# A routed mixture of experts: when rows are gathered, on GpSimd's queue, and four weight pieces in flight

## The chip, the cores and the metric

The kernel runs on one core of one Trainium2 chip. The metric is the device time of one execution in microseconds (us), lower is better. A core has five engines that matter here, each with its own instruction stream: TensorE (PE in the profile; PEld is its weight load), VectorE (DVE), ScalarE (ACT), GpSimd (POOL) and SyncE (SP). They meet at semaphores. Data move by DMA; SyncE issues those with fixed addresses, GpSimd those whose rows are picked by an index (gathers and scatters).

## The reference

Attention, then a mixture of experts on its result, then a feed-forward layer with a cosine:

```python
x = attention(q, k, v)                      # 2 x 768 tokens of 8 heads x 64 = 1536 x 512, a window of 16 and block sums
do_compute = x @ w_skip > 0                 # a token below is passed on as it is
logits = x[do_compute] @ w_gate             # 8 experts
e_idx, gate_w = argmax(logits), max(softmax(logits))
for e in range(8):                          # each token to one expert
    mask = e_idx == e
    y[mask] = gate_w[mask] * (relu(xc[mask] @ w1[e]) @ w2[e])    # 512 -> 1024 -> 512
x[do_compute] += y
h = x @ w_in                                # 512 -> 2048
out = (h * cos(h)) @ w_out                  # 2048 -> 512
```

All is float32. Which expert has how many tokens is known only on the chip. An expert's weights are two tiles of 2 MB.

## The kernel before

Attention goes first; beside it each tile of 128 tokens is routed, and its result rows are written to `xb`, an array in device memory. Then 36 small matmuls (`slots`, L575) sum, over the twelve tiles, which token stands in which slot of which expert; `slot_ids` makes the row indices of it. A slot that no token fills gets index 0.

An expert's tokens come in up to three gathers from `xb`. `xg` (`ex_gather`, with index `GIA`) is the first 32 rows, as 64 half rows of 256, 64 KB. `xo` (`ov_gather`, `GIS`) is 64 further rows of 512, 128 KB. `xm` (`many_gather`, `GIB`) is 128 further rows, 256 KB, gathered only inside a branch on the count, above 96. GpSimd issues all of them in program order through the helper `gather` (L623), and the scatters that write an expert's rows back through `scatter` (L627). The gathers of `xg0` and `xg1` go out ahead of the others. After the slots the program gathers `xg2`, `xo0`, `xm0`, `xg3`, `xo1`, `xm1`, and so on to `xo7`.

TensorE's order is fixed by the program. After the index work come the transposes of `xg0` (`turn_x`, L601), expert 0's first layer (`ex_w1`, L639), the remaining sums of `slots` (L575 again, 36 matmuls of three columns per expert), and the transposes of `xg1`. Small matmuls on a zero tile (`warm`, L169) stand at the program's start and ahead of the transposes of `xg0`. Then the loop over the experts: `ex_t` (transposes, and a copy on ScalarE), `ex_w1` of the next expert, `ex_x` (the transposes of `xg` of the one after that), `ex_w2` (L998), and `overflow`. `overflow` is a branch: above 32 tokens it transposes `xo` (L1014), above 96 it runs `full_tile` (L1058) on `xm`, and where a part is left `part_tile` (L1025) on `xo`. Between the experts gathers by `PERME` (`yload`) fetch finished rows for the last layer; the scatters of later experts into `xb` wait for these.

The weights come in pieces of 0.5 MB that SyncE issues (`load_piece`, L196), into a ring of eight 2 MB tiles. A piece waits until the piece three ahead of it (`AHEAD`, from the loop on five) has landed, or for a gather where one is given as `after`:

```python
        if after is None and len(pieces) >= ahead_of[-1]:
            after = pieces[-ahead_of[-1]]
        if after is not None:
            tc.add_manual_dep(d.ins, after.ins.name, SYNC, reason="pace")
```

After the experts comes the last layer (L1219 and on), TensorE work throughout.

Of the kernel before, what the change touches and what calls it, by code (L numbers as in the profile page):

```python
# [32 lines left out]
CAP = 32  # L33
XT = 128
YT = 64
# [84 lines left out]
def tile_kernel(ctx: ExitStack, tc: tile.TileContext, consts, qh, kh, vh, vw, w9, w1, w2, w_in, w_out, out):  # L120
# [44 lines left out]
    def warm(pool, tag, n, w=512):  # L165

        t = pool.tile([P, w], F32, tag=tag, name="warm")
        for _ in range(n):
            nc.tensor.matmul(t, wz[:, 0:P], wz[:, 0:w], start=True, stop=True)  # L169
# [506 lines left out]
    for u in range(4):  # L676
        load_w(u)
    warm(ps_t, "t", 27)
    warm(ps_t, "t", 12, 64)
    for i in range(NI - 1):  # L680
        fill, hot = (), None
        if i >= 8 and i % 2 == 0:
# [167 lines left out]
    slots(pib, lb, tail)  # L850
    slots(pic, lc, tail)
    warm(ps_s, "s", WN)
    warm(ps_s, "s", 56, 64)
    slot_ids(pib, idb)
    load_piece(slot_gi(idb, False, GIB), 1)
    slot_ids(pic, idc)
# [82 lines left out]

    xo = {}  # L940

    def ex_gather(e):
        xg.append(m1.tile([QA, 256], F32, name=f"xg{e}"))
        return gather(xg[e], GIA[:, e:e + 1], xb2)
# [11 lines left out]
    def many_gather(e):  # L956
        if e > 1:
            how_many(e)
        xm[e] = m2.tile([P, DM], F32, tag="xm", name="xm")
        with tc.If(cnts[e][0] > CAP + YT):  # L960
            apart(gather(xm[e], GIB[:, e:e + 1], xb), None, ("m", e % 2))

    def ex_x(e):
        xe[e] = m2.tile([P, P], F32, tag="xe", name="xe")
# [5 lines left out]
    def apart(d, to=None, key=None):  # L970

        for p, k in outs + inner:
            if key is None or k != key:
                tc.declare_no_dep(d.ins, p.ins, reason="every token has one slot of one expert")
        if to is not None:
            to.append((d, key))
        return d

# [3 lines left out]
    def ex_t(e):  # L982
        h = hs[e]
        pt = ps_l.tile([P, 2, P], F32, tag="p", name="pth")
        for s in range(2):
            nc.tensor.transpose(pt[:, s, :], h[:, s * P:(s + 1) * P], ident)
        hT = m2.tile([P, 2, P], F32, tag="hT", name="hT")
        nc.scalar.copy(out=hT, in_=pt)
        hs[e] = hT

    def ex_w2(e, hT, po, ns=range(8)):
# [306 lines left out]
    cv_load(0, 0, first_in)  # L1298
    load_piece(first_in)
    load_piece(ex_gather(2))  # L1300
    for e in range(2):
        load_piece(ov_gather(e))
        many_gather(e)
        load_piece(ex_gather(e + 3))
    for e in range(2, NE):
        if e + 3 < NE:
            load_piece(ex_gather(e + 3))
        load_piece(ov_gather(e))
        if e in (3, 5):
            cv_load(0, (e - 1) // 2)  # L1310
    while wq:
# [3 lines left out]
    for e in range(NE):  # L1315
# [4 lines left out]
        if e + 2 < NE:  # L1320
            ex_x(e + 2)
        do("B", e)
        if 0 < e < NE - 1:
            many_gather(e + 1)
        po = ps_g.tile([P, 256], F32, tag="g", name="po") if e == NE - 1 else ps_o.tile([P, 256], F32, tag="o", name="po")
# [205 lines left out]
```

## Time and profile before

| | us |
|---|---|
| median of 3 runs | 479.93 (478.94 to 479.98) |
| the profiled execution's own time | 479.16 |
| its span, first to last instruction | 477.2 |
| TensorE busy | 437.9 |
| VectorE, ScalarE, GpSimd busy | 301.2, 214.2, 142.5 |
| mean granted clock of TensorE | 0.977 |

The profile is of one execution, and times in it count from the first instruction. The time of a run is that of the whole execution, some 2 us more than the span. A row's idle time is that of its engine just ahead of the instruction, and the arrow names what ended it: an instruction of another engine, a DMA, an engine's own sequencer (PEq), or "issue", where nothing that is recorded ended it. "remote" is a signal whose sender the records don't give.

### The profile page before, as it was taken

To read this page: it belongs to the slowest core of one execution; us is meant where nothing else is said; L and a number is where in the kernel's file an instruction comes from. 1 tells how busy PE (TensorE), PEld (TensorE's weight loads), DVE (VectorE), ACT (ScalarE), POOL (GpSimd) and SP (SyncE) were. 2 spreads that over 40 slices of the span, in tenths; PEclk is the share of its full clock that TensorE was granted. 3 is DMA by queue.
4 is the path that set the end of the run, shared out by engine and by line. 5 is a ranking of instruction groups with operands and counts; after the bars stand their busy time and mean duration, and the time that the engine had idled before them with its cause. 6 is when DMAs were issued, how large, how long until landed. Compare 5 with 4: busy or idle time off the path is not lost.

```text
span 477.2 us, 9227 instructions
## 1 busy us (share of the span) xinstructions
PE 437.9 (92%) x3273; PEld 319.6 (67%) x3276; DVE 301.2 (63%) x842; ACT 214.2 (45%) x523; POOL 142.5 (30%) x170
## 2 busy tenths in 40 slices
PE   8899999509989897999999999999999999999994
PEld 4667676304444343567888888888888888888883
DVE  5697897106040051567679797998989956472831
ACT  2988993001332123346567566473646415051600
POOL 0755762650120024454053222231222100003043
PEclk9999999857999999999999999999999999999999
DMA  8999998799958389324312232321322000002021
GB/s 265 322 310 330 346 302 277 233 279 365 384 178 337 131 311 396 90 73 128 117 40 93 89 102 80 129 88 46 100 78 88 0 1 0 1 1 88 2 110 66
DMA packets 35180, 76.05 MB, mean 159 GB/s; under 512 B 4185, under 2 KB 10843, under 8 KB 35124
## 3 DMA queue, kind: packets, MB, share of 16 engines
q1 hardware_dynamic: 31876, 66.07, 42.2%
q0 software_dynamic: 3248, 9.27, 6.1%
q8 instruction: 31, 0.51, 0.5%
q14 instruction: 25, 0.20, 0.1%
HBM read 68.15 MB, written 7.60 MB: 159 GB/s over the span
## 4 chain that ended last, share of the span: by engine, by line
PE 29%; issue 18%; DVE 3%; POOL 3%; POOLq 0%; ACT 0%; DVEq 0%; ACTq 0%
PE pf L1219 14%; PE py L1398 11%; PE py L1464 2%; POOL out L627 2%; DVE g L1235 1%; PE pt L1144 1%; POOL wx L938 1%; DVE cvu L929 0%; DVE cvc L930 0%; DVE u L1225 0%; DVE c L1229 0%; POOLq L1527 0%; DVE nn L1224 0%; DVE cvu L927 0%; ACT u L1223 0%
## 5 line engine op out<-in xcount | busy, mean ns | idle before, releaser
L1219 PE MATMUL pf<-yb,wx 128*128 128x512 f32 x576 | 133.9, 390 | 1.3 <-DVE xg L1006 0.8
L1219 PEld LDWEIGHTS pf<-yb,wx 128*128 128x128 f32 x576 | 107.7, 188 | 24.2 <-PEq L1199 1.3
L1398 PE MATMUL py<-wx,g 128*128 128x512 f32 (+1 forms) x540 | 121.6, 384 | 0.0
L1398 PEld LDWEIGHTS py<-wx,g 128*128 128x128 f32 x540 | 99.9, 188 | 20.2
L1223 ACT ACTIVATE u<-pf,qbias 128x512 f32<-128x512 f32 x44 | 30.1, 685 | 78.2 <-PE pf L1219 78.0
L938 POOL TENSOR_TENSOR wx<-cvc,wx 128x512 fp32r<-128x512 f32 x24 | 34.7, 1446 | 94.7 <-ACT wx L937 91.5
L1404 DVE TENSOR_TENSOR ya<-py,ya 128x512 f32<-128x512 f32 (+1 forms) x37 | 23.8, 672 | 28.2 <-PE py L1398 26.2
L1235 DVE TENSOR_TENSOR g<-c,g 128x512 fp32r<-128x512 f32 x40 | 41.3, 1032 | 0.1
L336 ACT ACTIVATE sm<-sm,nm 128x128 f32<-128x128 f32 x96 | 37.4, 393 | 2.1 <-DVE nm L324 2.0
L1228 ACT ACTIVATE c<-u 128x512 f32<-128x512 f32 x44 | 27.6, 627 | 16.0 <-DVE g L1235 16.0
L627 POOL DMA_INDIRECT out<-ya,PERM x11 | 10.9, 992 | 79.9 <-DVE ya L1404 79.2
L1224 DVE TENSOR_SCALAR nn<-u 128x512 f32<-128x512 f32 x44 | 18.6, 424 | 23.1 <-ACT u L1223 23.0
L1225 DVE TENSOR_TENSOR u<-u,nn 128x512 f32<-128x512 f32 x44 | 30.5, 693 | 1.5
L1229 DVE TENSOR_TENSOR c<-pf,c 128x512 f32<-128x512 f32 x44 | 30.1, 684 | 0.7 <-ACT c L1228 0.7
L346 POOL TENSOR_TENSOR sm<-sm,su 128x512 f32<-128x512 f32 x23 | 24.2, 1050 | 21.3 <-DVE su L345 10.8
L324 DVE CUSTOM_DVE_ANT_0 sm<-sc,cst 128x128 f32<-128x128 f32 x96 | 23.6, 284 | 7.0 <-PE sc L317 6.0
L1234 ACT CAST g<-c 128x512 fp32r<-128x512 f32 x44 | 26.7, 607 | 0.2 <-DVE c L1229 0.2
L937 ACT CAST wx<-cvc 128x512 fp32r<-128x512 f32 x24 | 14.9, 622 | 16.1 <-DVE cvc L930 16.1
L1083 DVE SCALAR_TENSOR_TENSOR xm<-pox,GTB,xm 128x512 f32<-128x512 f32 x2 | 1.5, 750 | 30.4 <-PE pox L1073 30.4
L627 POOL DMA_INDIRECT xb<-xg,SIA x8 | 7.8, 978 | 41.9 <-DVEq L1199 15.5
L317 PE MATMUL sc<-kT,q 64*64 64x128 f32 x384 | 17.5, 282 | 2.3 <-DVE nm L324 1.4
L929 DVE SCALAR_TENSOR_TENSOR cvu<-cvc,cvu 128x512 int32<-128x512 int32 x24 | 17.5, 731 | 3.0 <-DVE cvu L927 0.5
(256 smaller groups left out, 631.5 us busy)
## 6 DMA issues: line engine op xcount, KB each, us to landing
w<-w SPq DMA_DIRECT2D x62, 512.0 KB
raw<-w_in SPq DMA_DIRECT2D x16, 512.0 KB
raw<-w_out SPq DMA_DIRECT2D x16, 512.0 KB
kT<-kh SPq DMA_DIRECT2D x8, 384.0 KB
vn<-vh SPq DMA_DIRECT2D x12, 256.0 KB
xb<-xtok SPq DMA_DIRECT2D x12, 256.0 KB
q<-qh SPq DMA_DIRECT2D x4, 512.0 KB
vt<-vw SPq DMA_DIRECT2D x12, 128.0 KB
```

The source lines that it names most:

```text
L336: nc.scalar.activation(out=sm[:, p, :], in_=sm[:, p, :], func=AF.Exp, scale=-1.0, bias=nm[:, p:p + 1], accum_out=su[:, p:p + 1])
L346: nc.gpsimd.tensor_tensor(out=sm, in0=sm, in1=su.unsqueeze(2).to_broadcast([P, NP, P]), op=ALU.mult)
L627: return nc.gpsimd.indirect_dma_start(out=dst, out_offset=bass.IndirectOffsetOnAxis(ap=idx, axis=0), in_=src, in_offset=None, bounds_check ...
L938: eng.tensor_tensor(out=lo, in0=c, in1=hi.bitcast(F32), op=ALU.subtract)
L1219: nc.tensor.matmul(p, w[:, k, fs], y[:, k, :], start=(n == 0), stop=(n == 11))
L1223: nc.scalar.activation(out=u, in_=p, func=AF.Identity, scale=1.0 / (2.0 * math.pi), bias=qbias)
L1225: nc.vector.tensor_tensor(out=u, in0=u, in1=nn, op=ALU.subtract)
L1228: nc.scalar.activation(out=c, in_=u, func=AF.Sin, scale=TWO_PI)
L1229: nc.vector.tensor_tensor(out=c, in0=p, in1=c, op=ALU.mult)
L1234: nc.scalar.copy(out=gh, in_=g)
L1235: (nc.gpsimd if i in POOL_G else nc.vector).tensor_tensor(out=gl, in0=g, in1=gh.bitcast(F32), op=ALU.subtract)
L1398: nc.tensor.matmul(p, a[:, ws], b[:, f, cs], start=(n == 0), stop=(n == 11))
```

## The change

Four things change. Twelve small warm-up matmuls move from ahead of the slots to the program's start. Among the gathers after the slots, `xg2`, `xg3` and `xg4` stay in a row with `xo1` and `xm1`, while `xg5`, `xg6` and `xg7` go out among the experts 1 and 2, behind the copy in `ex_t` (`begun`). `ov_gather` moves into `many_gather`, inside a branch on more than 32 tokens, an expert ahead of its use. The weight pieces after `xg3` wait only for other pieces, three back and then four back. Scatters no longer wait for gathers that are listed in `reads`, since no token has two slots.

```diff
-    warm(ps_t, "t", 12, 64)
+    warm(ps_t, "t", 24, 64)
...
-    warm(ps_s, "s", 56, 64)
+    warm(ps_s, "s", 44, 64)
...
+    begun = {}
+    reads = []
+
+    def behind(e, d):
+
+        if e > 0:
+            tc.add_manual_dep(d.ins, begun[e].ins.name, SYNC, reason="one expert after the other")
+        for p, _ in outs + inner:
+            tc.declare_no_dep(d.ins, p.ins, reason="every token has one slot of one expert")
+        reads.append(d)
+
...
         xm[e] = m2.tile([P, DM], F32, tag="xm", name="xm")
-        with tc.If(cnts[e][0] > CAP + YT):
-            apart(gather(xm[e], GIB[:, e:e + 1], xb), None, ("m", e % 2))
+        with tc.If(cnts[e][0] > CAP):
+            behind(e - 1, ov_gather(e))
+            with tc.If(cnts[e][0] > CAP + YT):
+                behind(e - 1, gather(xm[e], GIB[:, e:e + 1], xb))
...
         if to is not None:
+            for p in reads:
+                tc.declare_no_dep(d.ins, p.ins, reason="every token has one slot of one expert")
             to.append((d, key))
...
-        nc.scalar.copy(out=hT, in_=pt)
+        begun[e] = nc.scalar.copy(out=hT, in_=pt)
...
     load_piece(ex_gather(2))
-    for e in range(2):
-        load_piece(ov_gather(e))
-        many_gather(e)
-        load_piece(ex_gather(e + 3))
+    load_piece(ex_gather(3))
+    many_gather(0)
+    many_gather(1)
+    load_piece()
+    load_piece()
+    load_piece()
+    ahead_of.append(4)
     for e in range(2, NE):
         if e + 3 < NE:
-            load_piece(ex_gather(e + 3))
-        load_piece(ov_gather(e))
+            load_piece()
+        load_piece()
...
         do("B", e)
+        for g in {0: (4,), 1: (5,), 2: (6, 7)}.get(e, ()):
+            behind(e, ex_gather(g))
         if 0 < e < NE - 1:
             many_gather(e + 1)
```

The first place is on GpSimd, behind the slots. In the kernel before, from xg4 on (`xg_2092` is xg4, `xg_2095` xg5, `xo_2070` xo2, `xg_2100` xg6, `xo_2103` xo3, `xg_2108` xg7, `xo_2111` xo4, `xo_2114` xo5; the last row is xo6 and xo7, the scatter is that of expert 0):

```order
L623 DMA xg_2092<-xb,GIA 64x256
L623 DMA xg_2095<-xb,GIA 64x256
L623 DMA xo_2070<-xb,GIS 64x512
L623 DMA xg_2100<-xb,GIA 64x256
L623 DMA xo_2103<-xb,GIS 64x512
L623 DMA xg_2108<-xb,GIA 64x256
L623 DMA xo_2111<-xb,GIS 64x512
L623 DMA xo_2114<-xb,GIS 64x512
L623 DMA xo_2118<-xb,GIS 64x512 x2
L627 DMA xb<-xg_1774,SIA 3072x256
```

In the changed kernel, at the same place, from expert 1's branch on (L971 is the branch on 32 tokens, L973 that on 96; `xo_2069` is xo1, `xg_2157` xg4):

```order
L971 COMPARE_AND_BRANCH
L623 DMA xo_2069<-xb,GIS 64x512
L973 COMPARE_AND_BRANCH
L623 DMA xm<-xb,GIB 128x512
L973 UNCONDITIONAL_BRANCH
L973 ISA
L973 UNCONDITIONAL_BRANCH
L971 ISA
L971 UNCONDITIONAL_BRANCH
L623 DMA xg_2157<-xb,GIA 64x256
L627 DMA xb<-xg_1786,SIA 3072x256
```

After xg4 GpSimd goes on to the scatter of expert 0; nothing of the experts 5 to 7, and no `xo` of an expert beyond 1, stands ahead of it.

The second place is on GpSimd too, ahead of expert 5. In the kernel before, the last instruction of the scatters' branch of expert 3, the counts of expert 5 and the branch for its xm stand ahead of the scatter of xg4 (`xg_2092`):

```order
L1199 UNCONDITIONAL_BRANCH
L837 TENSOR_LOAD CNT x2
L960 COMPARE_AND_BRANCH
L623 DMA xm<-xb,GIB 128x512
L960 UNCONDITIONAL_BRANCH
L960 ISA
```

In the changed kernel (`xo_2912` is xo5), the same:

```order
L1214 UNCONDITIONAL_BRANCH
L837 TENSOR_LOAD CNT x2
L971 COMPARE_AND_BRANCH
L623 DMA xo_2912<-xb,GIS 64x512
L973 COMPARE_AND_BRANCH
L623 DMA xm<-xb,GIB 128x512
L973 UNCONDITIONAL_BRANCH
L973 ISA
```

The gather of xo5 has come from behind the slots to this place, behind the scatters of expert 3.

## Rows read from the trace of the kernel before

**Rows 1.** The page, part 1, first row: busy time, share of the span, instructions.

```profile
PE 437.9 (92%) x3273; PEld 319.6 (67%) x3276; DVE 301.2 (63%) x842; ACT 214.2 (45%) x523; POOL 142.5 (30%) x170
```

**Rows 2.** The page, part 4, first row: the chain that ended last, by engine.

```profile
PE 29%; issue 18%; DVE 3%; POOL 3%; POOLq 0%; ACT 0%; DVEq 0%; ACTq 0%
```

**Rows 3.** Stretch, length, busy PE, PEld, DVE, ACT, POOL; clock, DMA share, GB/s.

```profile
88.60:93.00 4.40, 1.40 (x26) 1.16 (x27) 0.00 (x0) 0.00 (x0) 3.18 (x5) 0.99 0.89 256
93.00:108.00 15.00, 1.76 (x12) 1.36 (x11) 0.10 (x1) 0.38 (x1) 8.74 (x10) 0.50 1.04 279
108.00:113.40 5.40, 5.40 (x48) 2.41 (x50) 3.45 (x26) 1.18 (x4) 0.00 (x0) 0.50 1.03 342
113.40:128.00 14.60, 14.26 (x127) 7.03 (x120) 5.63 (x25) 3.21 (x8) 1.95 (x2) 1.00 1.04 398
```

**Rows 4.** Timeline of TensorE (PE): start and length in us; idle before in brackets.

```profile
84.81 1.13 PE L169 MATMUL warm<-wz 128*128 128x64 bf16 x33
85.98 0.30 PE L601 MATMUL ptx<-ident,xg 64*128 64x64 f32 x2
86.64 1.93 PE L639 MATMUL ph<-w,cst 128*32 128x256 f32 x32 [0.35 <-ACT cst L602]
88.86 0.55 PE L575 MATMUL pia<-R,OR 128*64 128x24 bf16 x12 [0.29 <-issue]
...
99.34 0.18 PE L575 MATMUL pic<-R,OR 128*64 128x24 bf16 x1 [1.96 <-issue]
...
107.80 0.39 PE L601 MATMUL ptx<-ident,xg 64*128 64x64 f32 x2 [1.93 <-issue]
...
108.73 3.64 PE L639 MATMUL ph<-w,cst 128*32 128x256 f32 x32
...
115.24 0.41 PE L986 MATMUL pth<-ident,h 128*128 128x128 f32 x2 [0.19 <-PEq L1199]
115.58 1.93 PE L639 MATMUL ph<-w,xe 128*32 128x256 f32 x32
```

**Rows 5.** Waits of all engines, 86 to 112 us: total, times, longest us.

```profile
DVE s_ii L590 <- remote: 21.8, 1, 21.8
...
ACT cst L642 <- remote: 9.2, 1, 9.2
```

**Rows 6.** Timeline of GpSimd (POOL), 82 to 130 us.

```profile
82.27 1.12 POOL L623 DMA_INDIRECT xg<-xb,GIA  x1 [2.12 <-DMA w<-w]
...
86.50 0.91 POOL L623 DMA_INDIRECT xg<-xb,GIA  x1 [1.89 <-PE ptx L601]
...
103.57 0.91 POOL L623 DMA_INDIRECT xo<-xb,GIS  x1 [0.30 <-issue]
...
119.53 0.97 POOL L623 DMA_INDIRECT xm<-xb,GIB  x1 [1.22 <-issue]
128.02 0.95 POOL L627 DMA_INDIRECT xb<-xg,SIA  x1 [7.52 <-DMA xm<-xb,GIB]
```

**Rows 7.** All DMA, 90 to 108 us, then 110 to 126 us.

```profile
DMA packets 2048, 5.07 MB, mean 282 GB/s; under 512 B 302, under 2 KB 302, under 8 KB 2047
...
DMA packets 2333, 6.32 MB, mean 395 GB/s; under 512 B 219, under 2 KB 219, under 8 KB 2330
```

**Rows 8.** Timeline of TensorE, the start.

```profile
9.51 1.61 PE L317 MATMUL sc<-kT,q 64*64 64x128 f32 x32 [0.48 <-DMA q<-qh]
```

**Rows 9.** Timeline of TensorE at expert 5.

```profile
184.43 0.46 PE L1014 MATMUL ptx<-ident,xo 64*128 64x64 f32 x4
```

**Rows 10.** Timeline of GpSimd, 130 to 205 us.

```profile
174.76 0.96 POOL L623 DMA_INDIRECT xo<-xb,PERME  x1 [2.53 <-DVEq L1199]
183.29 0.92 POOL L627 DMA_INDIRECT xb<-xg,SIA  x1 [7.57 <-DMA xo<-xb,PERME]
186.59 0.92 POOL L627 DMA_INDIRECT xb<-xg,SIA  x1 [2.38 <-DVEq L1201]
```

**Rows 11.** Timeline of TensorE in expert 2's full tile.

```profile
143.43 4.56 PE L1058 MATMUL phx<-w,xx 128*128 128x512 f32 x10
```

## The prediction

> **What bounds the kernel now.** The page comes first: TensorE is busy for 437.9 of 477.2 us [rows 1], and the chain that ended last is mostly TensorE work, with 18% "issue", time in which an engine waited for nothing that the profile names [rows 2]. So the end is set by TensorE, and what counts is where it stands idle. The windows show one large hole: between 88.6 and 108 us it is busy for 3.16 of 19.4 us [rows 3], where the slots of the experts' tokens are made and expert 0 has only begun. From 93 to 113.4 the granted clock is 0.50, the lower of its two levels (1.2 of 2.4 GHz).
>
> The timeline of TensorE shows what is done in the hole: the 36 small matmuls of L575 [rows 4]. The first twelve run in 0.55 us; the later ones come singly, behind gaps such as the 1.96 us of "issue" at 99.34, until the transposes of xg1 at 107.80. At the cadence of the first twelve all 36 would take 1.65 us, so of the 19.2 us between the end of expert 0's first layer (86.64 + 1.93 = 88.57) and 107.80 about 17.6 are stall. The waits say the same of other engines [rows 5]: ScalarE takes the result of that layer 9.2 us late, VectorE waits 21.8 us.
>
> What runs beside it is GpSimd: 15 indirect gathers, one every 1.22 us, from 86.50 to 103.57 + 0.91 = 104.48 [rows 6]. TensorE is free 3.3 us after the last. The DMA engines move 282 GB/s in 90 to 108, against 395 in 110 to 126 [rows 7]. One gather alone does no harm: xm2 goes out at 119.53 [rows 6], and TensorE is busy for 14.26 of the 14.6 us from 113.4 to 128 [rows 3]. An empty slot has index 0, so it reads token 0. Counted from the reference's inputs the experts have 23, 131, 179, 9, 3, 60, 13 and 10 tokens; of the 1024 slots of these gathers 616 are empty. My reading: many gathers in a row, most of whose reads fall on one token, hold up the sequencers until they are through.
>
> **The change, part by part.** The sum is made against the profiled execution, 479.16 us (span 477.2); it is 0.77 under the median of the runs.
>
> *Warm-ups.* Twelve small ones more at the start, twelve fewer ahead of the slots. 33 of them take 1.13 us in the row at 84.81 [rows 4], so twelve are 0.41. At the start TensorE waits 0.48 us for q behind its warm-ups [rows 8], which covers them; without that cover they would cost 0.41. At the other place the transposes of xg0 follow with no wait named, so up to 0.41 is gained if xg0's data are there: between 0 and -0.4, I take **-0.2**.
>
> *The hole.* Ten of the 15 gathers leave it: xo0, xo3, xo4, xo6 and xo7 are skipped, xg5, xg6, xg7, xo2 and xo5 come later. xg2, xg3, xo1, xm1 and xg4 stay. By the lag, the fifth ends at 86.50 + 4 x 1.22 + 0.91 = 92.3, and TensorE is free 3.3 later, at 95.6 instead of 107.8: 12.2 gained. By number, 5/15 of 17.6 is 5.9 of stall left, 11.7 gained; by empty slots (133 of 616) 3.8 are left, 13.8 gained. I take **-12.2**, the middle one. Bounds: all of it, -17.6. At the other end, the weight pieces no longer wait for gathers and four are in flight instead of three, so the stream may run at its full rate beside the five; in such a stream xm2 took from 119.53 to 128.02, 8.5 us, until the scatter behind it could start [rows 6], and with 8.5 in place of 3.3 the gain is 7.0. That TensorE comes to the weights earlier costs nothing in these rows: none of its waits is one for w [rows 4, 9].
>
> *The clock.* The new hole, up to 95.6, takes in the point at which the clock fell, so I let the half-speed stretch move along. The first layer of expert 1 takes 3.64 us in it, that of expert 2 behind it 1.93 [rows 4]: 1.7 is what it costs there. Taken: **0**; bound -1.7, if the clock holds.
>
> *Expert 5's rows.* Only experts 1, 2 and 5 have more than 32 tokens. xo1 and xo2 are still gathered an expert ahead. But xo5 is now issued behind the scatter of xg3, which waits until 183.29 for a gather of finished rows by PERME that was issued at 174.76 [rows 10]. GpSimd is in order, so xo5 cannot go before 183.29 + 0.92 + 0.30 = 184.5; two reads of counts and two branches stand between, and in before the engine was through with such ones by 186.59. I take 185.0. TensorE takes xo5 at 184.43 [rows 9]; in before the last of the gathers had gone out 80 us earlier. What does the gather take? 64 KB: xg0, issued at 82.27 [rows 6], was there by 85.98, so at most 3.7. 256 KB: 8.5 (xm2, and 174.76 to 183.29 here). For 128 KB a straight line gives 3.7 + 64/192 x 4.8 = 5.3. TensorE would wait until 190.3: **+5.9**, with 184.5 + 3.7 and 186.6 + 8.5 as bounds, 3.8 to 10.7. Queued behind it on TensorE is everything to the end, in program order, so the chain moves by the whole wait.
>
> The Trainium skill ("DMA: Bandwidth & Descriptors", section "Anatomy of one DMA — SWDGE (gpsimd) path") puts a DMA that GpSimd issues at about 2.0 us plus its bytes at 436 GB/s. By it xo5 would take 2.3 us, as an estimate, the wait would be 2.9 and the sum 3.0 lower; xm2 would take 2.6 where the row has 8.5, with weights streaming beside it, so the rows decide.
>
> *The gathers that moved.* xg5, xo2 and xm2 go out in the stretch of expert 1 (xm2 did before), xg6 and xg7 in that of expert 2, behind two gathers of finished rows. On GpSimd they cost 1.22 each, ahead of scatters; the one at 128.02 waited 7.52 us there [rows 6], which hides them; without that cover four would cost 4.9. TensorE keeps 0.46 us per matmul (ten in 4.56) behind those two gathers now [rows 11]. **0**, up to +4 (third rival).
>
> *Branches.* Each engine has one more compare for each expert. A row of TensorE shows 0.19 us that its own sequencer ended at such a place [rows 4]: six behind the hole are 1.1 if none is hidden, nothing if the sequencer runs ahead of the array; nearer to the latter, **+0.3**. That scatters no longer wait for gathers takes no wait off TensorE in these rows: 0.
>
> Sum: 479.16 - 0.2 - 12.2 + 0 + 5.9 + 0 + 0.3 = 473.0 in the terms of this execution, 473.7 in those of the median; I say **473.5**.
>
> **The rivals.** *The stall is not the gathers' (slower).* VectorE is all but idle through the hole [rows 3], the gathers write tiles of their own, and no row names them as what TensorE waits for: "issue" names nobody. If the hole comes from something else that starts there, such as the weight stream, it stays, and xo5's wait is all that is new: 479.16 - 0.2 + 5.9 + 0.3 = 485.2. It decides where the hole gives back less than 6.0. Against it speak GpSimd's rows, whose end the hole follows, and the DMA rate. Chance 0.14. A rule of the Trainium skill would have it so: "SBUF — State Buffer", section "Who interferes with whom", says that DMA never contends with a compute engine, and that TensorE and ScalarE never wait on anyone. The trace disagrees so far as both stood still for 9 us and more beside the gathers, but names no culprit.
>
> *The hole closes wholly.* Five gathers, with 133 empty slots, may be too few to hold anything up, as xm2 was. Then 17.6 goes, the clock holds (-1.7), and xo5 may come at its lower bound: 479.16 - 0.4 - 17.6 - 1.7 + 3.8 + 0.3 = 463.6. Chance 0.12.
>
> *The hole comes again in expert 2.* xg6 and xg7 (38 and 44 of 64 half rows empty) make four gathers nearly back to back with the two of finished rows. If that starts the stall, it lasts for about 2 x 1.22 + 3.3 = 5.7 us, and at one matmul in two microseconds (99.34 [rows 4]) instead of 0.46 some 4 of them are lost: 477.0. Against it: the two there now did nothing. Chance 0.11.
>
> **How the numbers follow.** The forecast's own range, 470 to 476.5, has 0.55. The hole closed: 0.12, 461 to 466.5. The hole again in expert 2, or xo5 near its upper bound (+4.8, 477.8): 0.19 together, 476.5 to 481. The stall as it was: 0.14, 481.5 to 486. 466 to 481 leaves out some 0.2. A difference below 0.2%, 1 us, is about what a measurement of this kernel cannot tell: faster 0.83, same 0.03, slower 0.14.
>
> **What would show it.** In the changed kernel's profile: five gathers of GpSimd up to about 92, and the transposes of xg1 near 95.6, with few "issue" gaps of L575; near 107.8 if the stall is not the gathers', near 90 if it is gone. A stretch at 0.50 of the clock that ends some 5.6 us after the hole. At expert 5 a wait of TensorE for the gather of xo, of 3.8 to 10.7 us, where there was none, behind a scatter that ends just ahead of the gather. In expert 2 a cadence of 0.46 us. I am wrong if the hole's end doesn't follow GpSimd's last gather, or if xo5 is there before TensorE wants it.

## The result, and the profile after

The changed kernel is slower: 485.78 us median of 4 runs (485.51 to 486.65) beside 479.44 of the kernel before (478.80 to 479.98), a ratio of 1.0133 [1.0111, 1.0155]. The run after_2 further down gave 1.0138 [1.0092, 1.0185]. Medians here and below take in every run, while ratios leave out the runs that lie more than 1.5% above the fastest of their kernel (two of few_first_2 and one of tile_short_2). The forecast was 473.5, faster. The changed kernel's profiled execution took 486.65 us with a span of 484.8, that is 7.6 more than before.

The page of the changed kernel, its first row (beside [rows 1]):

```profile
PE 445.3 (92%) x3273; PEld 322.5 (67%) x3276; DVE 301.2 (62%) x842; ACT 214.0 (44%) x523; POOL 138.9 (29%) x165
```

The same 3273 matmul records are busy 7.4 us longer. A matmul lasts longer at the lower clock, so the first question is where that clock now lies. The windows of the changed kernel (columns as in [rows 3]):

```profile
93.00:98.00 5.00, 3.87 (x37) 2.29 (x41) 3.12 (x21) 1.02 (x3) 0.00 (x0) 0.50 1.02 278
...
107.00:111.00 4.00, 0.54 (x3) 0.30 (x3) 0.73 (x2) 0.65 (x2) 1.73 (x2) 0.87 1.03 373
111.00:115.00 4.00, 4.00 (x7) 1.93 (x7) 0.23 (x1) 0.37 (x1) 0.94 (x1) 0.50 1.04 307
...
191.00:194.00 3.00, 2.44 (x10) 0.97 (x10) 0.00 (x0) 0.37 (x1) 1.02 (x2) 0.50 0.14 38
```

The hole that began at 88.6 is shorter, but there is a new one from 107 to 111 (0.54 us of matmuls in 4), and the granted clock is 0.50 behind it and again at 191. TensorE's timeline in the changed kernel says what stands at these places:

```profile
85.98 0.30 PE L601 MATMUL ptx<-ident,xg 64*128 64x64 f32 x2 [0.35 <-DMA xg<-xb,GIA]
...
90.97 0.26 PE L575 MATMUL pib<-R,OR 128*128 128x24 bf16 x4 [1.20 <-issue]
...
94.37 0.47 PE L601 MATMUL ptx<-ident,xg 64*128 64x64 f32 x2
...
95.77 3.64 PE L639 MATMUL ph<-w,cst 128*32 128x256 f32 x32 [0.30 <-ACT cst L602]
...
106.50 0.43 PE L1029 MATMUL ptx<-ident,xo 64*128 64x64 f32 x4
106.86 0.44 PE L1064 MATMUL ptx<-ident,xm 128*128 128x128 f32 x2
110.77 0.69 PE L1064 MATMUL ptx<-ident,xm 128*128 128x128 f32 x2 [3.46 <-ACT xx L1031]
111.25 7.21 PE L1073 MATMUL phx<-w,xx 128*128 128x512 f32 x10
...
129.73 0.42 PE L1001 MATMUL pth<-ident,h 128*128 128x128 f32 x2
...
138.44 0.69 PE L1064 MATMUL ptx<-ident,xm 128*128 128x128 f32 x2 [3.54 <-ACT xx L1031]
138.91 7.03 PE L1073 MATMUL phx<-w,xx 128*128 128x512 f32 x10
...
182.02 3.40 PE L1013 MATMUL po<-w,hT 128*32 128x256 f32 x32 [2.92 <-ACT wx L937]
190.74 0.66 PE L1029 MATMUL ptx<-ident,xo 64*128 64x64 f32 x4 [5.32 <-DMA xo<-xb,GIS]
191.95 5.29 PE L1040 MATMUL phy<-w,xx 128*64 128x512 f32 x16 [0.56 <-ACTq L1216]
...
208.86 3.49 PE L1234 MATMUL pf<-yb,wx 128*128 128x512 f32 x14 [0.45 <-ACTq L1214]
```

The same instructions in the kernel before, as far as [rows 4, 9, 11] don't have them (its line numbers are some 15 lower):

```profile
119.57 0.53 PE L1014 MATMUL ptx<-ident,xo 64*128 64x64 f32 x4
...
120.99 4.56 PE L1058 MATMUL phx<-w,xx 128*128 128x512 f32 x10
136.82 0.42 PE L986 MATMUL pth<-ident,h 128*128 128x128 f32 x2
...
167.78 0.44 PE L986 MATMUL pth<-ident,h 128*128 128x128 f32 x2
...
200.73 1.65 PE L1219 MATMUL pf<-yb,wx 128*128 128x512 f32 x6 [0.45 <-ACTq L1199]
```

Subtracting starts gives how far the changed kernel is ahead at each place. It gains 13.43 at the transposes of xg1 (107.80 to 94.37) and still has 13.07 at xo1's (119.57 to 106.50). From there it gives all of it back:

| place | lost, us | what it is |
|---|---|---|
| expert 1's 128-row tile | 3.33 + 2.65 | a wait for `xx` L1031; then 7.21 in place of 4.56 for the first layer |
| expert 2's 128-row tile | 2.57 + 2.48 | the same: a wait of 3.54 (1.17 before); 7.03 in place of 4.56 |
| expert 5, second layer (`po` at 182.02) | 2.96 | late by 2.92, and 3.40 long |
| xo5 | 5.32 | the wait for its gather |
| behind it | 1.82 | mostly 5.29 in place of 3.65 for `phy` |

With 0.07 between these rows the losses are 21.2, so at the last layer (200.73 to 208.86) the changed kernel is 8.13 late; it makes up 0.5 before the end. The sum of the profile is thus closed. The question is what the first two rows of the table are.

GpSimd's timeline in the changed kernel:

```profile
86.69 0.90 POOL L623 DMA_INDIRECT xg<-xb,GIA  x1 [2.60 <-DVE GIS L585]
...
91.59 0.91 POOL L623 DMA_INDIRECT xg<-xb,GIA  x1 [0.30 <-issue]
104.36 0.97 POOL L627 DMA_INDIRECT xb<-xg,SIA  x1 [11.86 <-DVEq L1214]
105.64 0.92 POOL L623 DMA_INDIRECT xg<-xb,GIA  x1 [0.30 <-issue]
106.86 0.91 POOL L623 DMA_INDIRECT xo<-xb,GIS  x1 [0.30 <-issue]
108.08 0.96 POOL L623 DMA_INDIRECT xm<-xb,GIB  x1 [0.31 <-issue]
...
135.94 0.91 POOL L623 DMA_INDIRECT xg<-xb,GIA  x1 [0.30 <-issue]
...
183.62 0.92 POOL L623 DMA_INDIRECT xo<-xb,GIS  x1 [1.22 <-issue]
```

A scatter and the gathers of xg5, xo2 and xm2 now go out in one row from 104.36 to 109.04. TensorE's wait falls into it. What the others did, ScalarE's and then VectorE's timeline:

```profile
110.34 0.37 ACT L1031 COPY xx<-ptx 128x256 f32<-128x256 f32 x1 [5.47 <-remote]
```

```profile
110.23 1.00 DVE L1021 SCALAR_TENSOR_TENSOR xg<-po,GTA,xg 64x256 f32<-64x256 f32 x2 [4.73 <-remote]
```

VectorE waits for the last `po` matmul, which by TensorE's rows was through by 106.5; ScalarE waits for the transposes of xo1, through by 106.95 (the ends of matmuls are modelled, their starts are recorded). Both are released together, at 110.2 to 110.3, though what they wait for ended at different times. One slow transfer or matmul would not release both at once, so I read it thus: TensorE's finished work becomes visible late, 1.2 us after the last gather of the row. The hole of the kernel before shows the same on VectorE:

```profile
107.90 0.17 DVE L590 COPY s_ii<-pia 64x24 f32<-64x24 f32 x1 [21.79 <-remote]
```

This copy needs `pia`, whose last matmul was through at 88.86 + 0.55 = 89.41 [rows 4], 18.5 us earlier. The hole and the stalls in the tiles thus look like one thing. In the changed kernel expert 2 repeats the stall, with two gathers of finished rows, xg6 and xg7 from 131.95 to 136.85.

### The profile page after: what moved, and what is told of

Its sections match the earlier page's. It is cut to its first block, busy times and chain, and to the rows that moved or that the text cites. A ratio compares the mean times of both kernels' runs of the same rounds, so it can differ in the third digit from the quotient of the medians.

```text
span 484.8 us, 9238 instructions
## 1 busy us (share of the span) xinstructions
PE 445.3 (92%) x3273; PEld 322.5 (67%) x3276; DVE 301.2 (62%) x842; ACT 214.0 (44%) x523; POOL 138.9 (29%) x165
## 4 chain that ended last, share of the span: by engine, by line
PE 28%; issue 18%; DVE 3%; POOL 3%; POOLq 0%; ACT 0%; DVEq 0%; ACTq 0%
PE pf L1234 14%; PE py L1418 11%; PE py L1484 2%; POOL out L627 2%; DVE g L1250 1%; PE pt L1159 1%; POOL wx L938 1%; DVE cvu L929 0%; DVE cvc L930 0%; DVE u L1240 0%; DVE c L1244 0%; POOLq L1547 0%; DVE nn L1239 0%; DVE cvu L927 0%; ACT u L1238 0%
## 5 line engine op out<-in xcount | busy, mean ns | idle before, releaser
L627 POOL DMA_INDIRECT out<-ya,PERM x11 | 10.9, 988 | 79.9 <-DVE ya L1424 79.3
L346 POOL TENSOR_TENSOR sm<-sm,su 128x512 f32<-128x512 f32 x23 | 24.1, 1048 | 21.3 <-DVE su L345 10.9
L1073 PE MATMUL phx<-w,xx 128*128 128x512 f32 x32 | 19.7, 775 | 0.0
L1013 PE MATMUL po<-w,hT 128*32 128x256 f32 x256 | 16.9, 409 | 2.9 <-ACT wx L937 2.9
```

The costliest lines, as they stand in the source:

```text
L346: nc.gpsimd.tensor_tensor(out=sm, in0=sm, in1=su.unsqueeze(2).to_broadcast([P, NP, P]), op=ALU.mult)
```

## The experiments

All times are medians, us; each ratio is against the kernel before as it ran beside that kernel. The runs come in five groups. In the second (triple_mid, few_first, spaced, best1) and the fourth (tile_short, short_only, mid_small, mid_plain) the kernel before itself took 460.88 and 462.28, and it seems to have no hole there: no profile of it was taken in them, but in the kernels profiled there that keep its row of gathers (triple_mid, short_only, mid_small, mid_plain) the 36 small matmuls run through. No run here explains why (one chip showed both, 460.88 and 479.52). Ratios against 461 to 462 are not to be mixed with the others.

| run | time | before | ratio |
|---|---|---|---|
| xo5_early | 481.77 | 479.38 | 1.0043 [1.0024, 1.0062] |
| in_tile1 | 476.30 | 479.38 | 0.9945 [0.9922, 0.9968] |
| triple | 479.93 | 479.38 | 1.0017 [1.0001, 1.0032] |
| hold | 479.35 | 479.38 | 0.9995 [0.9983, 1.0007] |
| triple_mid | 465.13 | 460.88 | 1.0106 [1.0019, 1.0193] |
| few_first | 468.37 | 460.88 | 1.0166 [1.0105, 1.0227] |
| best1 | 462.89 | 460.88 | 1.0048 [1.0019, 1.0077] |
| spaced | 466.70 | 460.88 | 1.0114 [1.0048, 1.0179] |
| after_2 | 485.15 | 479.52 | 1.0138 [1.0092, 1.0185] |
| best1_2 | 468.53 | 479.52 | 0.9756 [0.9722, 0.9790] |
| few_first_2 | 477.99 | 479.52 | 0.9943 [0.9914, 0.9972] |
| triple_mid_2 | 482.37 | 479.52 | 1.0071 [1.0049, 1.0092] |
| tile_short | 471.42 | 462.28 | 1.0186 [1.0133, 1.0239] |
| short_only | 473.16 | 462.28 | 1.0251 [1.0201, 1.0330] |
| mid_small | 463.42 | 462.28 | 1.0008 [0.9973, 1.0044] |
| mid_plain | 463.05 | 462.28 | 0.9998 [0.9965, 1.0031] |
| mid_small_2 | 484.03 | 479.28 | 1.0094 [1.0063, 1.0124] |
| tile_short_2 | 480.50 | 479.28 | 0.9996 [0.9961, 1.0031] |

**The theory.** A row of indirect gathers holds TensorE wherever TensorE runs many short instructions, and does nothing beside long ones. The rivals: it is the empty slots, the stream of weights beside the gathers, the rows that they move, or xo5's wait alone.

The groups without the hole limit the theory from the start. mid_small is the kernel before up to its additions, which go out behind the row, at 105.77. TensorE's timeline there, then GpSimd's, then VectorE's:

```profile
90.41 0.55 PE L575 MATMUL pia<-R,OR 128*64 128x24 bf16 x12 [0.29 <-issue]
...
91.28 0.55 PE L575 MATMUL pic<-R,OR 128*64 128x24 bf16 x12
```

```profile
87.36 0.90 POOL L623 DMA_INDIRECT xg<-xb,GIA  x1 [2.16 <-DMA w<-w]
...
104.56 0.91 POOL L623 DMA_INDIRECT xo<-xb,GIS  x1 [0.30 <-issue]
```

```profile
90.99 0.17 DVE L590 COPY s_ii<-pia 64x24 f32<-64x24 f32 x1 [4.03 <-PE pia L575]
```

The same 15 gathers, 1.22 us apart, stand beside the same 36 short matmuls, and these run through by 91.83; VectorE has `pia` 0.03 us after it is done. So a row beside short instructions isn't enough. Something else has to come with it, which the groups differ in and no run shows; what follows holds for the groups with the hole.

### xo5 earlier (xo5_early)

The changed kernel, with xo5 gathered in expert 3's stretch.

```diff
-            behind(e - 1, ov_gather(e))
+            if e != 5:
+                behind(e - 1, ov_gather(e))
...
+        if e == 3:
+            how_many(5)
+            with tc.If(cnts[5][0] > CAP):
+                behind(3, ov_gather(5))
```

> The changed kernel (485.8 us) with one edit: xo5 is gathered in expert 3's stretch, behind the two gathers of finished rows and ahead of the scatter of xg3, some 8 us before TensorE wants it, not behind that scatter. In the changed kernel's trace TensorE waits 5.3 us for xo5 and its next 16 matmuls take 5.29 us in place of 3.65, at half clock. If the wait is what it seems, both go: 485.8 - 5.3 - 1.6 = 478.9. The gather is now the third in a row there; by the theory that bursts hold up TensorE it may cost up to 3 us again in expert 3 or 4: 479 to 482. If the wait for xo5 only covers another one (weights of expert 5), 484 or more.

The gather goes out at 173.81, and TensorE takes it at 187.16 with no wait, with `phy` back at 3.65. That wait and its clock are gone, but 3.01 us of "issue" ahead of 182.76 now stand in expert 5, where 2.92 stood in the changed kernel. Net it is 4.0 faster than 485.78, and still slower than before. The 478.9 expected if both go is missed: new waits of some 2 us stand ahead of xo5 (0.93 ahead of 169.03, and 1.06 for weights ahead of 184.09). The time lies in the 479 to 482 named for a row that costs again, but that the row makes these waits is not shown. xo5 is a part of the loss, not its core.

### The row of gathers beside long matmuls (in_tile1)

The changed kernel, with xo2, xm2, xg5, xg6 and xg7 in one row, inside expert 1's 128-row tile.

```diff
-        for g in {0: (4,), 1: (5,), 2: (6, 7)}.get(e, ()):
-            behind(e, ex_gather(g))
-        if 0 < e < NE - 1:
+        if e == 0:
+            behind(e, ex_gather(4))
+        if 1 < e < NE - 1:
             many_gather(e + 1)
...
+        if e == 1:
+            many_gather(2)
+            for g in (5, 6, 7):
+                behind(e, ex_gather(g))
         do("O", e)
```

> The changed kernel with xo2, xm2, xg5, xg6 and xg7 gathered in one row behind the scatter of expert 1, while TensorE is in expert 1's tile of 128 rows, instead of three ahead of that tile and two ahead of expert 2's. In the changed kernel's trace TensorE loses 6.0 us at the start of the first of these tiles and 5.0 at the start of the second, a gap of 3.5 us each and then half clock. Theory (gathers in a row hold up what TensorE signals to the other engines): both losses go, and a smaller one appears inside expert 1's tile, 0 to 5 us: 475 to 480. Rival (TensorE has caught up with its weights or rows, which come no earlier): the losses stay, 485 to 486.

A scatter and five gathers go out from 107.73 to 114.92, a longer row than the one that did the harm. TensorE's timeline in in_tile1, then ScalarE's:

```profile
107.98 4.56 PE L1073 MATMUL phx<-w,xx 128*128 128x512 f32 x10
112.43 0.66 PE L1081 MATMUL pgx<-ident,hx 128*128 128x128 f32 x4
```

```profile
111.78 0.60 ACT L1076 ACTIVATE hx<-phx 128x512 f32<-128x512 f32 x1 [3.32 <-issue]
```

The first half of the layer is eight of these ten, through at 107.98 + 8 x 0.456 = 111.63, and ScalarE has it at 111.78, in the middle of the row. This signal isn't late, the clock stays, and 485.78 becomes 476.30: 9.5 of the 11 us that the table lists for the experts 1 and 2. xo5's wait is still there (5.92).

### Which gathers, and which stream (triple, hold)

In triple the kernel before issues two more gathers behind xm2. In hold no weight piece is sent until the last gather of the first row has landed.

```diff
             apart(gather(xm[e], GIB[:, e:e + 1], xb), None, ("m", e % 2))
+            if e == 2:
+                for x in (ysrc[0], ysrc[3]):
+                    apart(gather(x, GIB[:, e:e + 1], xb))
```

```diff
+            ex_gather(e + 3)
+        last = ov_gather(e)
...
+            load_piece(last if e < 4 else None)
+        load_piece(last if e < 4 else None)
```

> The kernel before (479.4 us) with two more gathers right behind that of xm2, into tiles free at the time, with the indices of xm2: all 128 slots filled, no empty one. They do work that nothing needs. Theory (it is the number of gathers in a row, beside the weight stream): TensorE's transposes at the start of expert 1's tile are seen late by ScalarE, until about 1.2 us after the third gather, near 124; 3 to 4 us of gap and up to 2.6 of half clock: 482 to 486. Rival (it is the empty slots, which all read token 0): no stall, 479 to 480.

> The kernel before with the 15 gathers unchanged and the weight pieces after xg2 held back until the last gather (xo7) has landed, so that no weights stream beside the gathers. Theory in its plain form (gathers in a row hold up TensorE whatever else the DMA engines do): the transposes of xg1 stay near 107.8, 479 to 481. Rival (the gathers drain too slowly beside the stream, and their backlog does it): the 36 small matmuls run through, the transposes of xg1 come at 90 to 95, and the time falls to 463 to 470, if the held weights are not late for experts 2 and 3.

triple went against my expectation: three gathers at 119.56, 120.84 and 122.09 leave a gap of 0.15 us and 4.56 for the ten matmuls. They stand beside 512-column matmuls, and this turned the theory from "three in a row" to "beside what". In hold the hole is there as before, while the weights are away: the transposes of xg1 come earlier, one at 100.86 and one at 101.58, but expert 1's first layer behind them starts at 108.54 (108.73 in the kernel before). Its windows, then its DMA over the same stretch:

```profile
94.00:106.00 12.00, 1.99 (x10) 1.15 (x8) 0.00 (x0) 0.19 (x1) 8.09 (x9) 0.50 0.38 103
```

```profile
DMA packets 482, 1.23 MB, mean 103 GB/s; under 512 B 181, under 2 KB 181, under 8 KB 482
```

103 GB/s in place of 279 [rows 3], and TensorE is busy for 1.99 of 12 us. So the weight stream isn't the cause of the hole.

### The same gathers beside short matmuls (triple_mid, mid_small, mid_plain)

The kernel before, with three added gathers behind the copy of xg2's transposes, where TensorE runs 32-row matmuls. triple_mid moves 128, 64 and 64 rows (all of them filled slots), mid_small 16 filled ones each, mid_plain uses plain DMAs of weights from GpSimd. What the additions fetch isn't used; `cx` is the copy.

```diff
+        if e == 0:
+            how_many(2)
+            with tc.If(cnts[2][0] > CAP + YT):
+                for x, a, b in ((ysrc[0], 0, P), (ysrc[3], 0, YT), (ysrc[3], YT, P)):
+                    d = apart(gather(x[a:b], GIB[0:b - a, 2:3], xb))
+                    tc.add_manual_dep(d.ins, cx.ins.name, SYNC, reason="behind")
```

> The kernel before with three more gathers of filled slots (indices of xm2; 128, 64 and 64 rows, into tiles free at the time; work that nothing needs) behind the copy of xg2's transposes, where TensorE runs the many short matmuls of expert 0's second and expert 2's first layer. Three such gathers beside the 512-column matmuls of expert 1's tile cost nothing in the run before this one. Theory as it now stands (gathers in a row hold up TensorE's signals where it runs dense streams of short instructions): TensorE's updates come 1 to 4 us late there, a gap ahead of expert 1's transposes or second layer, 481 to 484. Rival (empty slots, which all read token 0, do the harm): no gap, 479 to 480.

> The kernel before with three gathers of filled slots more beside the short matmuls of experts 0 and 2, again. On the second chip they went out at 105.1, in a row with the 15 others, and it took 465.1 us beside 460.9. On a chip like the first they go out alone near 113: a gap of 1 to 4 us in TensorE, 481 to 484, if gathers of filled slots hold up its signals beside short matmuls; none, 479 to 480, if that takes empty slots.

> The three added gathers beside expert 0's short matmuls, but of 16 rows each (32 KB) in place of 128, 64 and 64; their result is not used. If it is GpSimd's issue of a row of gathers that holds TensorE, the stall ahead of the next transposes (2.60 us with full gathers) stays above 1.5 us and the time is 1.5 to 4 us above the kernel before. If it is the rows that are moved, the gap is below 0.5 us and the time is within 1 us of the kernel before.

> The three added transfers at the same place are plain DMAs from GpSimd of 128, 64 and 64 rows of weights, without indices; their result is not used. If only indexed rows hold TensorE, no gap above 0.5 us and the time within 1 us of the kernel before. If any transfer that GpSimd issues does, 1.5 to 3 us of gap and 1.5 to 4 us above the kernel before.

> The three added gathers of 16 rows each, beside expert 0's short matmuls, once more. If the kernel before shows its hole again (479 to 480), the added gathers stand alone behind the hole, as the full ones did in triple_mid_2, and tell what those could: a stall above 1.5 us and 480.5 to 484 if GpSimd's issue holds TensorE, below 0.5 us and 478.5 to 480.5 if the rows moved do. Without the hole (459 to 463) it tells nothing new.

In the groups without the hole the additions came right behind the gathers that were there, so triple_mid, mid_small and mid_plain tell nothing apart; the question of plain DMAs stays open. In the other two the three stand alone, behind the hole. TensorE in triple_mid_2, TensorE in mid_small_2, and GpSimd in mid_small_2:

```profile
112.15 1.93 PE L998 MATMUL po<-w,hT 128*32 128x256 f32 x32
116.69 0.41 PE L986 MATMUL pth<-ident,h 128*128 128x128 f32 x2 [2.60 <-PEq L1199]
```

```profile
112.53 1.93 PE L998 MATMUL po<-w,hT 128*32 128x256 f32 x32
117.75 0.41 PE L986 MATMUL pth<-ident,h 128*128 128x128 f32 x2 [3.29 <-PEq L1199]
```

```profile
113.42 0.86 POOL L623 DMA_INDIRECT xo<-xb,GIB  x1 [8.76 <-ACT xe L602]
...
115.74 0.84 POOL L623 DMA_INDIRECT cst<-xb,GIB  x1 [0.30 <-issue]
```

In mid_small_2 the matmuls are through at 114.46, and TensorE passes on at 117.75, 1.2 us after the last gather; in the kernel before it did so at once ([rows 4], 0.19 at 115.24). Gathers of 16 rows, none empty, hold TensorE no less than those of 64 and 128 (3.29 us beside 2.60). VectorE waits for the same `po` and starts 0.1 us ahead of TensorE in both kernels (117.64 and 116.58), so it was held too, and the count that the edit makes TensorE read is not what holds them. So for this stall it is neither empty slots nor the rows moved; what is left is GpSimd's indirect gathers one behind the other. The 484.03 is just above its 480.5 to 484, with half clock behind the stall again (2.88 in place of 1.93 at 118.09).

### Short matmuls where the long ones were (tile_short, short_only)

The test meant to decide: in_tile1's row of gathers, at the place where it did no harm, but the first layer of the 128-row tiles in four 128-column matmuls for each 512-column one. short_only makes that edit in the kernel before, as a control. In tile_short and short_only the four pieces each start the sum of a region that they share, so that this layer comes out incomplete; in tile_short_2 only the first does, and it is whole.

```diff
-                nc.tensor.matmul(ph[c], xx[:, k, :], wa[:, k, 512 * c:512 * c + 512], start=(k == 0), stop=(k == 3))
+                for q in range(4):
+                    nc.tensor.matmul(ph[c][:, P * q:P * q + P], xx[:, k, :], wa[:, k, 512 * c + P * q:512 * c + P * q + P],
+                                     start=(k == 0 and q == 0), stop=(k == 3), skip_group_check=True)
```

> The six gathers in a row stay in expert 1's 128-row tile, but the first layer of that tile (and of expert 2's) is written as 128-column matmuls, four in place of each 512-column one. If what matters is how short the instructions are that TensorE runs beside a row of gathers, TensorE's signals are late here: ScalarE takes the first half of the tile 1 us or more after the matmuls are through, TensorE stands for 1 to 4 us, and the time is 478 to 483. If what matters is the place (what TensorE waits for there) and not the length of its instructions, ScalarE takes it within 0.2 us as with the 512-column matmuls, TensorE has no gap above 0.5 us there, and the time is 475.5 to 478. Near 460 to 466 if the kernel before is in the state without the hole.

> The control of the one above: the kernel before with the same 128-column matmuls in both 128-row tiles, gathers where they were. What the shorter matmuls cost by themselves: 0 to 2 us over the kernel before, no gap above 0.5 us in either tile, whichever theory holds.

> Six gathers in a row in expert 1's 128-row tile, its first layer in 128-column matmuls, once more, against a kernel before that may show its hole. If short instructions are what a row of gathers holds, TensorE stands for 1 us or more in the first layer of that tile and the time is 478 to 483; if 0.12 us for a matmul is long enough, or the place is what counts, no gap above 0.5 us, and 475.5 to 478 (beside 476.3 with the 512-column matmuls). Without the hole: 461 to 472, and it adds nothing.

TensorE's timeline in tile_short_2, then ScalarE's:

```profile
108.58 1.26 PE L639 MATMUL ph<-w,xe 128*32 128x256 f32 x10 [2.65 <-issue]
...
114.61 4.73 PE L1074 MATMUL phx<-w,xx 128*128 128x128 f32 x40
121.04 0.66 PE L1083 MATMUL pgx<-ident,hx 128*128 128x128 f32 x4 [1.70 <-ACT hx L1078]
```

```profile
120.39 0.60 ACT L1078 ACTIVATE hx<-phx 128x512 f32<-128x512 f32 x1 [5.31 <-remote]
```

Thirty-two of the forty are the first half, through at 114.61 + 32 x 0.118 = 118.4. ScalarE has it at 120.39, 2.0 us later, with the gathers running from 116.00 to 121.87, and TensorE stands for 1.70. With 512-column matmuls it was 0.15. The place is the same and so is the row of gathers; the length of TensorE's instructions is what was changed, and this signal became late, though it came in the midst of the row and not behind its end as in the other stalls. That is for the theory, but weakly: tile_short, in the group without the hole and with the same row of gathers, has no such wait (phx at 107.39, the transposes behind it at 111.97), so short instructions beside the row don't suffice here either.

The total must not be read for this: 480.50 is 4.2 above in_tile1, while ten runs of this kernel lie between 476.68 and 484.42; the profiled one, 483.51, is among the longest, and 2.65 of it is the gap ahead of 108.58. It stands in the midst of one layer, with a single scatter beside it, and the two others with this edit have it too (2.15 in tile_short, 3.12 in short_only). In all three a 16 KB packet of an instruction queue starts 2.3 to 2.7 us before the gap ends. So it looks like TensorE's own instructions coming late; that wasn't tested by itself. The control missed its expectation by this: 10.9 above the kernel before, not 0 to 2. The gap of 3.12 and 3.16 in place of 1.93 for the `po` matmuls behind it are 4.4 of it; where the rest is I can't tell, since no profile of the kernel before without its hole was taken.

### Fewer gathers behind the slots, otherwise placed (few_first, spaced, best1)

few_first is the kernel before with `xo` at its old place, but only above 32 tokens. best1 is the changed kernel with xg4 to xg7, xo2 and xm2 in expert 1's tile and xo5 alone in expert 2's. spaced is best1 with memsets on GpSimd between the four gathers that are left behind the slots, xg3 the last of them.

```diff
+    def ov_if(e):
+        if e > 1:
+            c = cnt(0, e, NTOK)
+        else:
+            c = cnts[e][0]
+        with tc.If(c > CAP):
+            ov_gather(e)
```

```diff
+        if e == 2:
+            how_many(5)
+            with tc.If(cnts[5][0] > CAP):
+                behind(2, ov_gather(5))
+        if e == 1:
+            many_gather(2)
+            for g in (4, 5, 6, 7):
+                behind(e, ex_gather(g))
```

```diff
+    def spacer(n):
+        for _ in range(n):
+            nc.gpsimd.memset(ysrc[2], 0.0)
```

> The kernel before with one part of the change alone: a gather of xo only where its expert has more than 32 tokens, but at its old place behind the slots. Ten gathers stay in the row instead of 15 and none goes elsewhere, so expert 1's and 2's tiles and expert 5 keep their rows. If the hole lasts as long as the row of gathers, it ends 6 us earlier, near 101.7, and the time is 473 to 475 (a count's read and a branch between two gathers may stretch the row by 1 to 3 us: up to 477). If the harm is the empty slots': of 616 empty ones 296 are left, the hole ends near 97 and the time is 468 to 470.

> The kernel before with the gathers of xo under their branch, at their old place, again (468.4 us beside 460.9 on the second chip, where TensorE had a gap of 4.6 us ahead of expert 0's transposes that no run of the kernel before needs). On a chip like the first: the hole ends with the tenth gather, 473 to 477. On one like the second: 468.

> The kernel of the run above with work of GpSimd that nothing needs (two fills of a 128x512 tile) between the four gathers behind the slots, and xg3 last of them. Theory (gathers in a row do it, one alone does not): the 36 small matmuls run through, the transposes of xg1 come at 90 to 91, some 3 us earlier than in the run above, at full clock: 462 to 465. Rival (each gather beside the short matmuls holds TensorE up by itself): no better than the run above, or worse by the time that the fills stretch the row, 467 to 471.

> The changed kernel with xg4 to xg7, xo2 and xm2 gathered while TensorE is in expert 1's tile (512-column matmuls), and xo5 alone in expert 2's tile; four gathers stay behind the slots. From the run with that place for five of them (476.3 us), in whose trace TensorE waits 5.9 us for xo5 and then loses 2.0 to half clock: 476.3 - 5.9 - 2.0, and 1.2 for xg4 out of the first row: 467.2. If six or seven gathers in a row hold TensorE up even there, 470 to 474.

> The kernel with four gathers behind the slots, six in expert 1's tile and xo5 in expert 2's, again (462.9 us beside 460.9 on the second chip). On a chip like the first: the hole of four gathers (near 93 for the transposes of xg1) and no loss in the tiles, 466 to 469 beside 479.4. On one like the second: 461 to 464 beside 460.9.

> The changed kernel again, beside the kernel before on the chip of this call. The kernel before took 479.4 us on the chip of the first experiments and 460.9 on that of the second, where the 36 small matmuls run through, 17.6 us less as its hole would give. On a chip like the first: 485.8. On one like the second there is no hole to win, and what the change adds is left: the wait for xo5 and the half clock behind it, 5.3 + 1.6, and what the moved gathers cost in experts 1 and 2 there, 0 to 5: 467 to 473, slower than before.

after_2 repeats the result. Its profile has the two waits again, 3.50 and 3.42. few_first_2 shortens the hole, which ends at 100.05 with nine of its ten gathers gone out, but TensorE then stands for 4.69 us of "issue" ahead of the transposes at 105.21 (4.60 in few_first), and 477.99 misses its 473 to 477. In that gap stand TensorE's own reads of the added counts, six at 0.29 to 0.31 us, with the branches on them; that they are all of it wasn't tested. spaced loses at another end: xg3, issued last at 94.08, is waited for until 101.07 (3.36); on spacing it says nothing, since in best1 beside it the small matmuls run through without it. best1 shows that there is nothing to win where the hole is absent. Where it is there, best1_2 beats both kernels: 468.53 beside 479.52 and 485.15. TensorE in best1_2:

```profile
93.43 0.47 PE L601 MATMUL ptx<-ident,xg 64*128 64x64 f32 x2
...
106.69 4.56 PE L1074 MATMUL phx<-w,xx 128*128 128x512 f32 x10
...
172.39 0.69 PE L1030 MATMUL ptx<-ident,xo 64*128 64x64 f32 x4
```

Four gathers are left behind the slots, and the hole ends 0.9 earlier; six run beside the 512-column matmuls of expert 1 and cost nothing; nobody waits for xo5.

## Why the prediction was wrong

- **The step that failed** is "The gathers that moved", which I set at 0, "up to +4 (third rival)". The mechanism of that rival came, and in two places where I had looked at one: 3.33 and 2.57 us of standing, and 2.65 and 2.48 of half clock behind it, 11.0 in all. I had counted gathers in a row only behind expert 1, and taken the two gathers of finished rows that "now did nothing" for proof; the rival priced its stall without the clock that falls behind it. With these gathers at another place (in_tile1) the same change is 0.55% faster than before. So the loss is tied to where they go out; how a row of them holds TensorE stays open.
- **The hole** was right, and a little better: 13.4 against 12.2. It ends at 94.37, 1.9 after the last of five gathers (92.50), where I had put 95.6, and the "issue" gaps of L575 are few. The start of expert 1's first layer, steadier from run to run than xg1's transposes, says the same: 94.45 with four gathers behind the slots (best1_2), 95.77 with five, 108.3 to 109.1 with fifteen. So the hole's length follows the row wherever there is a hole; that the row alone makes it is what mid_small speaks against. hold takes away the weights as its cause. My reading that reads of one token hold up the sequencers fails for the stall of mid_small_2, where no slot is empty; for the hole it wasn't tested.
- **The slower rival** named 485.2, which is nearly the time measured. It isn't what happened: it kept the hole, and the hole shrank.
- **xo5** was right in kind, and its size, 5.32 against 5.9, is partly luck. The gather took 7.1 us from issue to use, not 5.3; TensorE came to it at 185.42, late by the 2.96 of the second layer, without which it would have waited some 8.3. By the Trainium skill ("DMA: Bandwidth & Descriptors", section "Anatomy of one DMA — SWDGE (gpsimd) path") it would have taken 2.3, as an estimate. The trace is nearer to the rows. What I left out is the half clock behind the wait, 5.29 in place of 3.65 for `phy`.
- **Expert 5's second layer**, 2.96, stood in no step. TensorE's own count reads (180.7 to 181.4) and a branch on them stand near the end of the wait, and a 16 KB packet of an instruction queue started at 178.26, 0.8 us ahead of its start. xo5_early keeps the gap without xo5's wait. Its cause is open.
- **Warm-ups**: -0.2 was taken, nothing came. The transposes of xg0 stand at 85.98 as before, now with a wait of 0.35 for the data.
- **The clock behind the hole** moved along as I said: 3.64 for the first layer of expert 1, at 0.50.

The Trainium skill ("SBUF — State Buffer", section "Who interferes with whom") has TensorE and ScalarE wait for nobody's use of the memory. In these runs both waited for signals: from 106.95 on they stood for some 3.4 us beside a row of gathers that produces nothing they need. Whether memory has a part in it, and so whether the rule is touched, no run here shows.

What stays open: why the kernel before has no hole in two of the groups, what delays TensorE's signals, why the same row of gathers holds TensorE in one group and not in another, and whether plain DMAs from GpSimd would do it too. That long instructions are spared rests on in_tile1, triple and best1_2, that short ones are held at the same place on one pair (in_tile1, tile_short_2). A rival that was not tested is that TensorE's own instructions come late: a 16 KB packet of an instruction queue starts near 93.7, in the midst of the hole of the kernel before. The 18.5 us by which VectorE sees finished work late speak against it as the whole cause.

## What to carry to other kernels

Before you move a row of indirect gathers, look at what TensorE runs at the new place, and measure there: beside 512-column matmuls six in a row cost nothing in any run here; beside 32-row matmuls and transposes three cost some 3 us in the groups with the hole and the half clock behind the stall up to nearly as much again, while in the groups without it a row of 15 cost nothing that shows. Price a stall of TensorE together with the slower stretch behind it, and a gather that goes out behind a waiting scatter with its whole way from issue to use (7.1 us here). When a profile shows waits of several engines that end together although what they wait for ended at different times, look for what else ended just before.

## What the runs showed of the hardware

- Beside a row of GpSimd's indirect gathers other engines took TensorE's finished work some 3.4 to 3.8 us late (changed kernel: through by 106.4 and 106.95, taken at 110.23 and 110.34) and 18.5 us late in the hole of the kernel before. Signals of work that ended at different times then came within about 0.1 us, which speaks for late signals and not for slow matmuls. In the groups without the hole the same row did none of it (mid_small: 0.03 us).
- Larger gathers didn't make it longer: three of 32 KB held TensorE for 3.29 us, one of 256 and two of 128 KB for 2.60, one kernel each.
- Reads of counts into registers are not free on TensorE: where few_first adds six of them, at 0.29 to 0.31 us each, and the branches on them, it stands for 4.6 to 4.7 us.
